# A gated linear-attention layer and its SiLU MLP under a new instruction planner: a modelled transfer queue and PE clock, idle matmuls in thin stretches, four load ranks, four units fed to the MLP one by one

## The chip, the cores and the metric

The kernel runs on one core of one Trainium2 chip. The metric is device time in microseconds (us) of one launch, as the median of several runs. The profile is of one further execution of the same program.

## The reference

There are 4 batches, 8 heads, 768 steps and a head width of 48. Everything is float32 outside the kernel.

```python
f = 1.0 / (1.0 + np.exp(-f_logit))
state = np.zeros((B, H, D, D), dtype=np.float32)
for t in range(S):
    state = f[:, :, t, :, None] * state + np.einsum('bhd,bhe->bhde', k[:, :, t], v[:, :, t])
    y[:, :, t] = np.einsum('bhd,bhde->bhe', q[:, :, t], state)
x = np.ascontiguousarray(y.transpose(0, 2, 1, 3)).reshape(B * S, H * D)   # 3072 x 384
h = x @ w_in                                                              # 384 -> 2048
out = (h * (1.0 / (1.0 + np.exp(-h)))) @ w_out                            # 2048 -> 384
```

The recurrence is computed in chunks of 128 steps, with cumulative sums of the log gates instead of a loop over time.

## The kernel before

**Units.** A unit `u` is one chunk of 128 steps of one batch, all 8 heads; there are 6 chunks times 4 batches, so 24 units, and unit `u` needs the state that unit `u-4` left. Two neighbouring units make a pair `P`, so 12 pairs.

**Steps of a unit**, by the names that the planner gives them (the line is that of the instruction in the kernel before):

- `f k q v` (L390): the four loads, issued by SP. `E`, `L` (L397, L399, ScalarE): log gates from `f`, for both units of a pair at once from pair 2 on.
- `cs` (L445, L449, TensorE): cumulative sums. `ia`, `al`, `a` (L452, L456, L454, ScalarE): three exponentials of them.
- `ki` (L458, GpSimd): k times `ia`. `qg` (L462, VectorE): q times `a`. `vb` (L460, GpSimd): v in bf16.
- the transpose of both: for units 0 to 7 `tq` on TensorE (L468) and a copy `qkc` on VectorE (L470), from unit 8 on `qkD`, a transposing transfer issued by SP (L472).
- `sc` (L479): scores, `at` (L483, VectorE): masked, `y` (L488, L492): the output of the unit, `yc` (L496, VectorE): in bf16.
- its transpose into `xT`: `yT` and `xc` (L502, L504) for units 0 to 7, `xD` from unit 8 on (a transposing transfer, SP, L498).
- `d`, `sd`, `su` (L510, L515 or L517, L521): the next state, on TensorE, VectorE, GpSimd.

**Steps of a pair in the MLP.** `mi` (L426) is a first product: 2 of 16 column tiles of `w_in` for 256 rows, 6 matmuls; 8 of them for a pair. `si` (L422, ScalarE) takes the SiLU of each into `hT`. `mo` (L436) is a quarter of the second product of one unit, 4 matmuls with 128 rows; 4 of them for a unit, in order. `oc` (L439, VectorE) copies the result and `so` (L442) stores it, from GpSimd's queue, for the last units from SP's. `wi` and `wo` (L409, L412) are the weight loads, four quarters each, issued from GpSimd's queue.

**What sets the order.** Nothing is left to a scheduler on the chip. `make_tasks` lists the steps with a duration each, their inputs and their buffers; `schedule` plays them through a model of the engines at build time and picks, on each engine, the ready step with the lowest rank (`pace` times the unit plus the rank of the step's kind). `planned` sorts the steps by the start that the model gave, and they are emitted in that order inside `tc.manual_schedule()`. So each engine runs its own list strictly in order, and waits at the head of the list whenever the model was too hopeful. Buffers are assigned by the model too (`SLOTS`): the PSUM class `mlp`, which holds the results of `mi` and `mo` and of the idle matmuls, has 3 buffers; `cs`, `sc`, `tq` and `yd` have one each.

**ScalarE's two tables.** `exp`/`ln` steps and `si` steps need different function tables, so an `ACT_TABLE_LOAD` is emitted wherever the list changes kind. `hold_...` and `keep_...` are the model's rules for when to change.

**Idle matmuls.** `warm` (L414) multiplies a zero tile into an `mlp` buffer. Before, 70 of them have the lowest priority from the start on, so they fill TensorE's first gaps, and the last is planned ahead of unit 0's `yT`.

**Weights.** `w_after=(2, 2, 2, 3, 3, 3, 4, 5)` ties each of the eight weight loads to the `ki` of a unit.

Of the kernel before, what the change touches and what calls it, by code (L numbers as in the profile page):

```python
# [21 lines left out]
NTILES = 16  # L22

CFG = dict(
    turned=8,
    turned_y=8,
    warm=70,
    warm_at=5.0,
    single=0,
    w_after=(2, 2, 2, 3, 3, 3, 4, 5),  # L30
    pace=3.66,
    margin=0.2,
    late_store=18,
    keep_exp=117.43,
    keep_silu=245.53,
    hold_exp=0.58,
    hold_silu=0.64,
    rank=dict(ld=-44.14, E=-215.27, cs=-365.49, ia=97.44, ki=-23.12, vb=175.4, qg=451.56, tq=-142.94, qkc=-77.52, sc=-74.11, at=-79.38, y=-7.63, yc=-223.81, yT=-176.78, xc=-369.47, d=13.22, sd=-254.14, su=26.79, mi=-117.59, si=-4.81, mo=20.95, mstep=0.47, oc=215.45, so=524.34, wi=23.7, wo=55.81),
# [5 lines left out]
ENGINES = ("PE", "ACT", "DVE", "POOL", "SP")  # L44
SEM = {"PE": 0.22, "ACT": 0.06, "DVE": 0.06, "POOL": 0.08, "SP": 0.0}
INTO_PE = 0.09
TABLE = 1.29


class Task:  # L50
    def __init__(self, name, eng, occ, lat, prio, deps=(), acq=(), use=(), mode=None, dma=0.0):
        self.name, self.eng, self.occ, self.lat, self.prio = name, eng, occ, lat, prio
        self.deps, self.acq, self.use, self.mode, self.dma = list(deps), list(acq), list(use), mode, dma
# [6 lines left out]

def make_tasks(cfg):
    T, tasks, pace, R = {}, [], cfg["pace"], cfg["rank"]
    extra = cfg.get("extra", {})

    def add(name, eng, occ, lat, prio, **kw):
        t = Task(name, eng, occ, lat, prio + extra.get(name, 0.0), **kw)
        T[name] = t
        tasks.append(t)
        return t
# [8 lines left out]
    base = lambda u: pace * u  # L78
    for n in range(cfg["warm"]):
        add(("warm", n), "PE", 0.107, 0.107, 1e6 + n, acq=[inst(("wm", n), "mlp")])  # L80
    for u in range(UNITS):
        P = u // 2
        for n, x in enumerate("fkqv"):
            add((x, u), "SP", 0.45, 0.45, base(u) + R["ld"] + n * 0.1, acq=[inst((x, P), x)], dma=0.875)

    for P in range(PAIRS):
        us_list = [(2 * P,), (2 * P + 1,)] if P < 2 else [(2 * P, 2 * P + 1)]
        for us in us_list:
            occ, lat = (0.43, 0.54) if len(us) == 1 else (0.74, 0.85)
            e = add(("E", us), "ACT", occ, lat, base(us[0]) + R["E"], deps=[T["f", u] for u in us], acq=[inst(("e", us), "e")],  # L90
                    use=[I["f", P]], mode="exp")
            add(("L", us), "ACT", occ, lat, base(us[0]) + R["E"] + 0.1, deps=[e], acq=[inst(("lf", P), "lf")],
                use=[I["e", us]], mode="exp")
    log_of = lambda u: T["L", (u,)] if u < 4 else T["L", (u - u % 2, u - u % 2 + 1)]

    for u in range(UNITS):
        c, b, P, B = u // BATCHES, u % BATCHES, u // 2, base(u)
# [5 lines left out]
        occ = 0.162 + (0 if last else 0.1)  # L103
        cs = add(("cs", u), "PE", occ, occ, B + R["cs"], deps=[log_of(u)], acq=[I["cs", u]], use=[I["lf", P]])
        ia = add(("ia", u), "ACT", 0.387, 0.49, B + R["ia"], deps=[cs], acq=[I["ia", u]], use=[I["cs", u]], mode="exp")
        if not last:
            al = add(("al", u), "ACT", 0.08, 0.173, B + R["ia"] + 0.1, deps=[cs], acq=[I["al", u]], use=[I["cs", u]], mode="exp")
        a = add(("a", u), "ACT", 0.387, 0.486, B + R["ia"] + 0.2, deps=[ia], use=[I["cs", u]], mode="exp")
        ki = add(("ki", u), "POOL", 0.94, 0.994, B + R["ki"], deps=[ia, T["k", u]], acq=[I["qk", u]], use=[I["ia", u], I["k", P]])
        vb = add(("vb", u), "POOL", 0.445, 0.503, B + R["vb"], deps=[T["v", u]], acq=[I["vb", u]], use=[I["v", P]])  # L110
        qg = add(("qg", u), "DVE", 0.47, 0.554, B + R["qg"], deps=[a, T["q", u]], acq=[I["qk", u]], use=[I["cs", u], I["q", P]])
        if u >= cfg["turned"]:
            qkT = add(("qkD", u), "SP", 0.6, 0.6, B + R["tq"], deps=[qg, ki], acq=[I["qkT", u]], use=[I["qk", u]], dma=1.3)
        else:
            tq = add(("tq", u), "PE", 0.444, 0.444, B + R["tq"], deps=[qg, ki], acq=[I["tq", u]], use=[I["qk", u]])
            qkT = add(("qkc", u), "DVE", 0.61, 0.692, B + R["qkc"], deps=[tq], acq=[I["qkT", u]], use=[I["tq", u]])
        sc = add(("sc", u), "PE", 0.425, 0.33, B + R["sc"], deps=[qkT], acq=[I["sc", u]], use=[I["qkT", u]])
        at = add(("at", u), "DVE", 1.2, 1.29, B + R["at"], deps=[sc], acq=[I["atm", u]], use=[I["sc", u]])
        yd = [at, vb] + ([T["su", u - BATCHES]] if c else [])
        y = add(("y", u), "PE", 0.38 if c else 0.21, 0.38 if c else 0.21, B + R["y"], deps=yd, acq=[I["y", u]],  # L120
                use=[I["atm", u], I["vb", u], I["qkT", u]] + ([I["st", u - BATCHES]] if c else []))
        yc = add(("yc", u), "DVE", 0.475, 0.558, B + R["yc"], deps=[y], acq=[I["yb", u]], use=[I["y", u]])
        if u >= cfg["turned_y"]:
            xc = add(("xD", u), "SP", 0.4, 0.4, B + R["yT"], deps=[yc], acq=[I["xT", P]], use=[I["yb", u]], dma=0.6)
        else:
            yT = add(("yT", u), "PE", 0.167, 0.167, B + R["yT"], deps=[yc], acq=[I["yT", u]], use=[I["yb", u]])
            xc = add(("xc", u), "DVE", 0.27, 0.358, B + R["xc"], deps=[yT], acq=[I["xT", P]], use=[I["yT", u]])
        T["x", u] = xc
        if not last:
            d = add(("d", u), "PE", 0.168, 0.168, B + R["d"], deps=[ki, vb, y], acq=[I["d", u]], use=[I["qk", u], I["vb", u]])  # L130
            sdd = [d] + ([T["su", u - BATCHES]] if c else [])
            sd = add(("sd", u), "DVE", 0.464, 0.551, B + R["sd"], deps=sdd, acq=[I["sd", u]],
                     use=[I["d", u]] + ([I["st", u - BATCHES]] if c else []))
            add(("su", u), "POOL", 1.01, 1.07, B + R["su"], deps=[sd, al], acq=[I["st", u]], use=[I["sd", u], I["al", u]])

    for n in range(4):
        add(("wi", n), "POOL", 0.8, 0.8, R["wi"] + n, deps=[T["ki", cfg["w_after"][n]]], dma=2.36)
    for n in range(4):
        add(("wo", n), "POOL", 0.8, 0.8, R["wo"] + n, deps=[T["ki", cfg["w_after"][4 + n]]], dma=2.5)

    for P in range(PAIRS):
        B = base(2 * P + 1)
        single = P < cfg["single"]
        for j in range(NTILES // 2):
            us = [(2 * P + i,) for i in range(2)] if single else [(2 * P, 2 * P + 1)]
            pass
        parts = [(2 * P,), (2 * P + 1,)] if single else [(2 * P, 2 * P + 1)]
        per = 4 if single else 2
        done = {}
        for us in parts:  # L150
            for j in range(NTILES // per):
                h = inst(("h", us, j), "mlp")
                deps = [T["x", u] for u in us] + [T["wi", (j * per) // 4]]
                off = 0.0 if len(us) == 2 else (us[0] - 2 * P - 1) * pace
                mi = add(("mi", us, j), "PE", 0.655, 0.655, B + off + R["mi"] + j * R["mstep"] * per / 2, deps=deps,
                         acq=[h], use=[I["xT", P]])
                done[us, j] = add(("si", us, j), "ACT", 0.476, 0.597, B + off + R["si"] + j * R["mstep"] * per / 2, deps=[mi],
                                  acq=[I["hT", P]], use=[h], mode="silu")
        for i in range(2):
# [3 lines left out]
            for m in range(4):  # L163
                need = [done[us, m]] if single else [done[us, 2 * m], done[us, 2 * m + 1]]
                mo = add(("mo", u, m), "PE", 0.648, 0.648, B + R["mo"] + (4 * i + m) * R["mstep"],
                         deps=need + [T["wo", m]] + ([T["mo", u, m - 1]] if m else []), acq=[o], use=[I["hT", P]])
            oc = add(("oc", u), "DVE", 0.468, 0.552, B + R["oc"] + 4 * i, deps=[mo], acq=[inst(("ob", u), "o")], use=[o])
            late = u >= cfg["late_store"]
            add(("so", u), "SP" if late else "POOL", 0.35 if late else 0.58, 0.5, B + R["so"] + 4 * i, deps=[oc], use=[I["ob", u]],
                dma=0.6)  # L170
# [3 lines left out]
def schedule(tasks, slots, cfg, fixed=None):  # L174

    margin = cfg["margin"]
    for i, t in enumerate(tasks):
        t.idx, t.start, t.end, t.succ, t.ready, t.left = i, None, None, [], 0.0, len(t.deps)
    for t in tasks:
        for d in t.deps:  # L180
            d.succ.append(t)
        for x in dict.fromkeys([*t.acq, *t.use]):
            x.users, x.slot = 0, None
    for t in tasks:
        for x in dict.fromkeys([*t.acq, *t.use]):
            x.users += 1
    free = {c: [(0.0, s) for s in range(n)] for c, n in slots.items()}
    busy = dict.fromkeys(ENGINES, 0.7)
    busy["PE"], busy["ACT"], busy["POOL"] = 1.3, 2.0, 1.9
    waiting = {e: [t for t in tasks if t.eng == e and not t.deps] for e in ENGINES}  # L190
    at = dict.fromkeys(ENGINES, 0)
    st = dict(mode="exp", last=2.0)
    ring = {"SP": [], "POOL": []}
# [386 lines left out]
```

## Time and profile before

| what | value |
|---|---|
| median of 3 runs | 204.59 us (204.46 to 205.04) |
| the profiled execution | 205.16 us |
| its span, first to last instruction | 203.3 us |
| TensorE busy (matmuls, overlapping ones counted once) | 179.0 us |
| ScalarE, VectorE, GpSimd busy | 121.3, 87.3, 72.5 us |
| mean granted TensorE clock | 0.938 |
| moved by DMA | 32.80 MB, 161 GB/s over the span |
| `ACT_TABLE_LOAD` | 16, 1283 ns each |

How to read it: "busy" counts a matmul from its start to its modelled end, and consecutive matmuls overlap, so 179.0 us is more than TensorE needs for this work at full speed. What a group of matmuls really costs is read from the chain of waits, where 60 `mi` matmuls in a row took 6.55 us and 24 `mo` matmuls 3.90 us: 0.655 us for one `mi` step of 6, 0.65 us for one `mo` step of 4. The profiled execution took 205.16 us, 1.86 us more than its span and 0.57 us more than the median of the runs.

### The profile page before, as it was taken

The page shows a single profiled execution, that of the slowest core. Times are in us where ns is not written, and L with a number is a line of the kernel's source. Part 1 is how long each engine was busy: PE and PEld are TensorE (multiplying, and loading weights), DVE is VectorE, ACT ScalarE, POOL GpSimd, SP SyncE. Part 2 cuts the span into 40 slices and gives each one's busy share as a digit, 9 for nine tenths or more (in the row PEclk, how much of TensorE's full clock was granted, in tenths as well). Part 3 has the DMA queues.
Part 4 walks back from the last instruction along what each step waited for, and adds up shares of the span by engine and source line. Part 5 has one row for each costly group of instructions (what it writes and reads, how often), then busy time and mean ns, then how long its engine had stood idle before and what let it go on. Part 6 is the DMA issues. An engine that isn't in the chain of part 4 may idle for free.

```text
span 203.3 us, 4480 instructions
## 1 busy us (share of the span) xinstructions
PE 179.0 (88%) x1766; PEld 131.1 (64%) x1766; DVE 87.3 (43%) x170; ACT 121.3 (60%) x208; POOL 72.5 (36%) x122
## 2 busy tenths in 40 slices
PE   7985889946999999969998997669979999999992
PEld 5764568734687678648567864438748678867850
DVE  4279261037264753872723064233845561162021
ACT  4646228962278769867739966186759767801700
POOL 2449603152181573383047004491167151000000
PEclk9997579995599999999999999969999999999998
DMA  6999999999999699999897999889899294003012
GB/s 133 204 193 173 191 189 195 204 200 187 204 221 236 120 166 247 197 185 191 175 221 156 161 194 187 188 187 213 160 234 156 80 115 112 0 16 118 25 42 77
DMA packets 129140, 32.80 MB, mean 161 GB/s; under 512 B 123904, under 2 KB 128256, under 8 KB 129120
## 3 DMA queue, kind: packets, MB, share of 16 engines
q1 hardware_dynamic: 124256, 25.83, 70.2%
q0 software_dynamic: 4864, 6.69, 14.8%
q8 instruction: 14, 0.23, 0.5%
q14 instruction: 6, 0.05, 0.1%
HBM read 25.17 MB, written 4.72 MB: 147 GB/s over the span
## 4 chain that ended last, share of the span: by engine, by line
PE 57%; DMA 13%; SPq 6%; ACT 3%; issue 2%; DVE 2%; POOL 0%; DVEq 0%; ACTq 0%
PE mlp L426 26%; PE mlp L436 23%; DMA f<-in_f_logit_dram 5%; SPq L390 5%; DMA xT<-yb 4%; DMA w_out_sb<-in_moe_w_out_dram 3%; PE sc L479 2%; PE yd L488 2%; ACT e L397 1%; PE yd L492 1%; PE cs L445 1%; SPq L498 1%; DVE qk L462 1%; DVE o L439 1%; PE yd L510 1%
## 5 line engine op out<-in xcount | busy, mean ns | idle before, releaser
L422 ACT ACTIVATE hT<-mlp 128x512 bf16<-128x512 f32 x96 | 56.6, 597 | 27.9 <-PE mlp L426 23.9
L436 PE MATMUL mlp<-w_out_sb,hT 128*128 128x384 bf16 x384 | 71.6, 333 | 1.8 <-DMA w_out_sb<-in_moe_w_out_dram 1.8
L426 PE MATMUL mlp<-xT,w_in_sb 128*128 128x256 bf16 x576 | 69.9, 280 | 2.7 <-DMA xT<-yb 1.3
L426 PEld LDWEIGHTS <-w_in_sb 128*128 128x128 bf16 x576 | 56.6, 100 | 12.6 <-DMA xT<-yb 2.0
L483 DVE TENSOR_TENSOR atm<-sc,triu 128x512 bf16<-128x512 f32 x48 | 30.9, 685 | 45.0 <-PE sc L479 44.8
L436 PEld LDWEIGHTS <-hT 128*128 128x128 bf16 x384 | 35.4, 99 | 22.8 <-issue 3.3
L458 POOL TENSOR_TENSOR qk<-k,ia 128x384 bf16<-128x384 f32 x24 | 23.9, 997 | 29.8 <-ACT al L456 22.2
L452 ACT ACTIVATE ia<-cs 128x384 f32<-128x384 f32 x24 | 11.7, 489 | 26.4 <-PE cs L449 20.5
L460 POOL CAST vb<-v 128x384 bf16<-128x384 f32 x24 | 12.0, 503 | 42.4 <-DMA v<-in_v_dram 29.5
L521 POOL TENSOR_TENSOR st<-sd,al 48x192 bf16<-48x192 f32 x40 | 20.1, 502 | 18.5 <-DVE sd L515 9.6
L462 DVE TENSOR_TENSOR qk<-q,cs 128x384 bf16<-128x384 f32 x24 | 13.2, 550 | 24.3 <-ACT cs L454 23.5
L439 DVE COPY o<-mlp 128x384 f32<-128x384 f32 x24 | 13.2, 554 | 18.6 <-PE mlp L436 18.5
L549 ACT ACT_TABLE_LOAD x15 | 19.2, 1283 | 0.3
L397 ACT ACTIVATE e<-f 128x768 f32<-128x768 f32 (+1 forms) x14 | 10.5, 750 | 14.6 <-DMA f<-in_f_logit_dram 14.6
L445 PE MATMUL cs<-lf,triu 128*128 128x384 bf16 x24 | 8.1, 339 | 9.9 <-DVE qk L462 6.6
L496 DVE CAST yb<-yd 128x384 bf16<-128x384 f32 x24 | 13.3, 552 | 6.7 <-PE yd L492 5.1
L449 PEld LDWEIGHTS <-lf 128*128 128x128 bf16 x80 | 5.0, 98 | 12.3 <-issue 10.7
L442 POOL DMA_DIRECT2D out_dram<-o x18 | 10.4, 580 | 5.3 <-DVE o L439 4.1
L454 ACT ACTIVATE cs<-cs 128x384 f32<-128x384 f32 x24 | 11.4, 477 | 0.6
L515 DVE TENSOR_TENSOR sd<-yd,st 128x384 f32<-128x384 f32 x16 | 8.8, 552 | 6.9 <-issue 2.9
L479 PE MATMUL sc<-qkT 48*128 48x128 bf16 x192 | 10.4, 233 | 1.1 <-DVE qkT L470 1.0
L414 PE MATMUL mlp<-idle 128*128 128x256 bf16 x70 | 10.1, 299 | 1.1 <-DVE idle L533 1.1
(35 smaller groups left out, 112.3 us busy)
## 6 DMA issues: line engine op xcount, KB each, us to landing
f<-in_f_logit_dram SPq DMA_DIRECT2D x24, 192.0 KB, 3.9
k<-in_k_dram SPq DMA_DIRECT2D x24, 192.0 KB, 4.1
q<-in_q_dram SPq DMA_DIRECT2D x24, 192.0 KB, 4.0
v<-in_v_dram SPq DMA_DIRECT2D x24, 192.0 KB, 4.0
out_dram<-o POOLq DMA_DIRECT2D x18, 192.0 KB, 3.7
w_in_sb<-in_moe_w_in_dram POOLq DMA_DIRECT2D x4, 384.0 KB, 9.1
w_out_sb<-in_moe_w_out_dram POOLq DMA_DIRECT2D x4, 384.0 KB, 9.5
out_dram<-o SPq DMA_DIRECT2D x6, 192.0 KB, 2.0
```

The source lines that it names most:

```text
L397: nc.scalar.activation(e, at("f", u // 2)[:, i:i + n], AF.Exp, scale=-1.0)
L422: return nc.scalar.activation(at("hT", P)[:, per * j:per * (j + 1), lo:hi], h, AF.Silu)
L426: nc.tensor.matmul(h[:, i, :], w_in_sb[:, kk, n * 128:(n + 1) * 128], at("xT", P)[:, kk, lo:hi], start=(kk == 0), stop=(kk == KT - 1))
L436: nc.tensor.matmul(o, at("hT", P)[:, n, i * C:(i + 1) * C], w_out_sb[:, n, :], start=(n == 0), stop=(n == NT - 1))
L439: nc.vector.tensor_copy(at("ob", u), at("o", u)[:, 0:d_model])
L458: nc.gpsimd.tensor_mul(at("qk", u)[:, 1, :, 0:D], at("k", P)[:, i], at("ia", u))
L462: nc.vector.tensor_mul(at("qk", u)[:, 0, :, 0:D], at("q", P)[:, i], at("cs", u)[:, 0:HD].rearrange("p (h d) -> p h d", d=D))
L479: nc.tensor.matmul(a_ps[:, r, p, :], qkT[lo:lo + D, 1, p, :], qkT[lo:lo + D, 0, p, :], start=True, stop=True)
L483: nc.vector.tensor_mul(at("atm", u)[:, r], at("sc", u)[:, r], triu[:, None, :].to_broadcast([C, NP, C]))
L496: nc.vector.tensor_copy(at("yb", u), at("y", u))
L521: nc.gpsimd.tensor_mul(at("st", u)[lo:lo + D, :, r * D:(r + 1) * D], at("sd", u)[lo:lo + D, :, r * D:(r + 1) * D], at("al", u)[lo:lo + D, ...
L549: nc.scalar.preload_act_table_set(tables[turn[id(t)]])
```

## The change

The arithmetic, the tiles, the buffers and the bytes moved are the same. The planner is replaced, and with it the order of every engine's list. Its core:

```diff
 CFG = dict(
-    turned=8,
-    turned_y=8,
-    warm=70,
-    warm_at=5.0,
-    single=0,
-    w_after=(2, 2, 2, 3, 3, 3, 4, 5),
-    pace=3.66,
-    margin=0.2,
+    single_logs=2,
+    single=2,
     late_store=18,
...
+    turned=range(8, 24),
+    turned_y=range(8, 24),
+    rank=dict(ldf=-50.7, ldk=16.34, ldq=10.3, ldv=40.31, E=114.29, cs=24.58, ia=-464.65, ki=-1093.0, vb=499.5, qg=-627.06,
...
+    rel={"wi_0": 23.29, "wi_1": 19.57, "wi_2": 16.93, "wi_3": 17.83, "wo_0": 14.71, "wo_1": 26.85, "wo_2": 38.7, "wo_3":
+         41.24},
+    pace=31.54,
...
+LOAD = dict(ring=0, svc=0.95, elig=1.2, land=0.75)
+QKD = dict(ring=0, svc=1.25, elig=1.25, land=1.1)
...
-            add((x, u), "SP", 0.45, 0.45, base(u) + R["ld"] + n * 0.1, acq=[inst((x, P), x)], dma=0.875)
+            add((x, u), "SP", 0.62, 0.62, "ld" + x, u, off=n * 0.1, acq=[inst((x, u // 2), x)], dma=LOAD)
...
-        if u >= cfg["turned"]:
-            qkT = add(("qkD", u), "SP", 0.6, 0.6, B + R["tq"], deps=[qg, ki], acq=[I["qkT", u]], use=[I["qk", u]], dma=1.3)
+        if u in cfg["turned"]:
+            qkT = add(("qkD", u), "SP", 1.25, 1.25, "qkD", u, deps=[qg, ki], acq=[I["qkT", u]], use=[I["qk", u]], dma=QKD)
...
-        add(("wi", n), "POOL", 0.8, 0.8, R["wi"] + n, deps=[T["ki", cfg["w_after"][n]]], dma=2.36)
+        add(("wi", n), "POOL", 0.8, 0.8, "wi", off=n, dma=W_IN)
...
+    def wants_warm():
+        if WARM_FROM <= now < WARM_ALL:
+            return True
+        past = now - win
+        return now < WARM_TO and clock > 0.6 and past > 0.8 and load_of(win, now) < WARM_SHARE * past
...
+        while win + WINDOW <= now + 1e-9:
+            share = load_of(win, win + WINDOW) / WINDOW
+            clock = 1.0 if share >= UP else 0.5 if share <= DOWN else clock
+            win += WINDOW
```

The constants are the planner's own; they act on the chip only through the order they lead to. That order, read from the two built programs:

- **SP.** Before, the loads go unit by unit as `f k q v`. After, they go by four ranks: `f:0 f:1 q:0 f:2 k:0 v:0 q:1 f:3 k:1 v:1 q:2 f:4 k:2 v:2 q:3 f:5 k:3 v:3 q:4 f:6 k:4 v:4 ...`, so `f` runs two units ahead of `k` and `v`, and `q` one. Before, the last load `v:23` is issued ahead of `xD:17`; after, in a steady pattern such as `f:17 k:15 v:15 q:16 f:18 xD:13 k:16 v:16 qkD:15 q:17 xD:14 qkD:16`, and the last load `v:23` stands behind `qkD:22` and `xD:20`.
- **GpSimd.** Weight loads before: `... vb:2 wi:0 wi:1 wi:2 ki:3 su:0 wi:3 wo:0 su:1 wo:1 vb:3 su:2 su:3 vb:4 vb:5 ki:4 wo:2 ki:5 vb:6 wo:3`. After: `... ki:1 vb:1 wo:0 ki:2 vb:2 su:0 wi:2 wi:3 su:1 wi:1 ki:3 su:2 wi:0 wo:1 vb:3 su:3 ki:4 vb:4 wo:2 ki:5 wo:3`.
- **ScalarE.** `E L ia al a` of unit 4 now come ahead of the first table load. There are 19 table loads between the kinds instead of 15: from pair 4+5 to pair 18+19 ScalarE changes to the exponentials and back around the 8 `si` steps of every pair, where before pairs 10+11 and 12+13 shared one stretch, and so did the last three pairs (after, the last two do).
- **TensorE.** 77 idle matmuls instead of 70, the last of them ahead of unit 3's `tq`. Units 0 to 3 pass the first product one by one (`single=2`): 4 steps each of 12 matmuls with 128 rows, in the order in which the quarters of `w_in` are asked for. From pair 8+9 on the list repeats, as here: `cs:17 y:15 sc:16 mo:12,0 d:12 mo:12,1 mo:12,2 mo:12,3 mo:13,0 mo:13,1 cs:18 y:16 mi:14+15,0 mi:14+15,1 d:13 mo:13,2 mo:13,3 mi:14+15,2 mi:14+15,3 mi:14+15,4 sc:17 mi:14+15,5 mi:14+15,6 mi:14+15,7 cs:19 y:17 ...`.

## Prediction before the run

> **What bounds the kernel now.** I first read the page's 40 slices, one digit for each 5.08 us.
>
> ```profile
> PE   7985889946999999969998997669979999999992
> ...
> PEclk9997579995599999999999999969999999999998
> DMA  6999999999999699999897999889899294003012
> ```
>
> TensorE looks busy nearly everywhere, DMA until slice 31. But the clock falls to half around 18 to 28 us and 46 to 56 us, and DMA's busy share is no proof of saturation: the page's GB/s row moves between 120 and 247 in those slices. So I asked how much of TensorE's time is work at full rate. The chain of waits gives prices where matmuls follow each other without a gap, and the places where they do not:
>
> ```profile
> 31.14 6.55 PE mlp L426 x60
> 37.69 3.90 PE mlp L436 x24
> ...
> 43.43 6.76 DMA w_out_sb<-in_moe_w_out_dram
> ...
> 86.11 5.03 DMA xT<-yb
> ...
> 101.08 3.18 DMA xT<-yb
> ...
> 128.53 3.48 DMA f<-in_f_logit_dram
> ```
>
> A `mi` step of 6 costs 0.655 us and a `mo` step of 4 costs 0.65; other rows of the chain give `cs` 0.24, `sc` 0.33, `y` 0.37 to 0.48 (I take 0.40), `d` 0.17 to 0.28 (0.2), `tq` 0.45, `yT` 0.17. A pair from unit 8 on is 8 x 0.655 + 8 x 0.65 + 2 x 1.17 = 12.8 us of TensorE. Between the first `mi` of pair 4+5 (58.21 us) and that of pair 22+23 (186.34 us) lie 72 `mi` and 72 `mo` steps (47.2 + 46.8) and the small steps of 18 units (20.8): 114.8 us of work in 128.1 us, so 13.3 us lost, in the DMA waits above and in waits for a late `f`. The three waits in the chain from 86 us on are of one sort: SP's list is in order, and what is needed next stands behind something that is waiting, or behind loads that nobody needs yet. Ahead of 58 us the view by windows (columns: length, PE busy, clock, DMA share, GB/s) shows the other loss:
>
> ```profile
> 42.00:46.00 4.00, 1.59 (x23) 0.85 1.01 195
> 46.00:50.00 4.00, 2.31 (x28) 0.50 1.22 190
> 50.00:54.00 4.00, 3.76 (x24) 0.50 1.27 215
> ...
> 152.00:186.30 34.30, 34.30 (x341) 1.00 0.48 89
> ```
>
> From 37.7 to 58.2 us TensorE does 11.7 us of work (12 `mo`, four `cs`, two each of `tq`, `sc`, `y`, `yT`, one `d`): it runs out of work at 41.6, waits for the third quarter of `w_out`, then works at a clock of 0.50. From 152 us on it is full at clock 1.00 while DMA has half its load or less: a backlog that the first 150 us left. The kernel is bound by TensorE, starved of inputs for its first three quarters.
>
> **The change, part by part.** I sum against the profiled execution, 205.16 us: 203.30 of span and 1.86 around it, 0.57 above the median.
>
> *Weights and start.* The first `mi` runs at 22.05 now, on a quarter of `w_in` issued at 15.21 (6.8 us to landing, the shortest of its four). In the new list `wi:2`, the first one needed, stands behind `vb:2` and `su:0`. `v:2` is the 14th load instead of the 12th, and `wo:0` (twice a load's bytes) goes ahead of it: four load times of 0.90 us (the 11 load issues from 34.95 to 44.88 us) after `vb:2`'s 14.76, then `su:0` for 1.1: issue near 19.5, landing 26.3 to 28.6 us. So the first products start 4 to 6 us later. They then have 16 steps, 10.5 us: end 37 to 40 us, against 37.69; I take 39. In that gap only 77 instead of 70 idle matmuls, 0.107 us each at full rate, keep the clock; I count no gain.
>
> *Single first products.* 12 matmuls of 128 rows take the place of 6 of 256. No row shows them; the nearest is `tq`, 8 transposes with a new weight tile each in 0.45 us, so 0.67 us a step, +0.2 us over 16 steps. The upper bound is one weight load each, not overlapped (99 ns): 1.19 us a step, +8.5 us. A gain is excluded, since the same columns stream. I take the `tq` row, which has the same shape; and part of it would hide behind the arrival of `w_in`.
> The Trainium skill speaks against this edit: "TensorE: Matmul & The Clock Gate", section "Back-to-back issue gap", gives about 81 ns for 128-column matmuls in a stream of load and matmul. By it the 16 steps would cost 16 x (12 x 0.081 - 0.655) = 5 us more instead of 0.2, an estimate. The trace's 56 ns a transpose is below that, so I stay with the row.
>
> *The third and fourth quarter of `w_out`.* Now issued at 43.43 and 46.12, behind `ki:4` and `ki:5`, which wait for the table change and `cs:4`. In the new list ScalarE does unit 4's exponentials ahead of the SiLUs, so `ki:4`, `vb:4` wait only for their loads. `v:4` is the 22nd load; the 20th and 24th landed by 35.9 and 39.5 us (the two `vb` rows that waited for them) behind the same number of weight quarters, six. So `wo:2` goes out near 38.2, `wo:3` after `k:5` near 42.2; landing 45.0 and 49.0 by the 6.8 us row. TensorE has 6.7 us of work from 39 on (6 `mo`, two each of `tq`, `cs`, `sc`, one each of `y`, `d`, `yT`); at 45.7 the third quarter is there, three `mo`, a `y` and a `cs` take it to 48.3, the fourth comes at 49.0, and after three `mo` and a `yT` pair 4+5 can begin at 51.1. If the thin stretch halves the clock again, as the window rows show, add 2 to 3 us. I take 52.7 against 58.21: a gain of 5.5, bounds 0 and 7.
>
> *The steady list.* Each pair now has its turn of exponentials and its turn of SiLUs. ScalarE's bill for a pair: 8 SiLUs of 0.60, two units of 0.49 + 0.17 + 0.48, `E` and `L` of 0.84, two table loads of 1.28: 11.3 us, under TensorE's 12.8. The four added table loads cost 5.1 us of ScalarE, hidden behind the `mo` steps of the pair before. If that cover goes, a pair costs up to 1.3 us more. What a table change costs beyond the load:
>
> ```profile
> 116.44 1.91 ACT L422 ACTIVATE hT<-mlp 128x512 bf16<-128x512 f32 x3
> 118.37 1.28 ACT L549 ACT_TABLE_LOAD   x1
> 119.66 0.84 ACT L397 ACTIVATE e<-f 128x768 f32<-128x768 f32 x1
> ```
>
> The next activation starts 0.01 us after the load, so 1.3 us in all.
> The Trainium skill ("ScalarE: Activation LUTs", "What ACT_TABLE_LOAD costs") puts a switch at about 2.66 us with a drain. By that, as an estimate, ScalarE would need 14.1 us for a pair and the sum below would rise by 9 x (14.1 - 13.4) = 6 us. The rows above show no drain.
>
> The new wait: `cs` of the even unit stands on TensorE behind six `mo` steps and needs the `L` of the same turn; behind it are queued that pair's `y` and `mi`, and ScalarE's SiLUs wait for these. The rows "cs waits for lf" hold 3.4 us in 6 cases, 0.57 each; one a pair for 9 pairs is 5.1 us. Where the old losses go: `f` is issued two units earlier than its `k` and `v`, so the waits for `f` should end; `xD` and `qkD` have fewer unneeded loads ahead. What is late next is `xD`: issued after `yc`, median 3.4 us to landing (2.3 to 5.0), and in the list some 4 us of other TensorE work lie between.
>
> SP's own bill for a pair is bounded: 8 loads of 0.6 and four transposing issues of 1.3 make 10.0 us of pure issue; with loads at the 0.90 us that the transfers took and two stores at the same price it is 14.2. I take 12.4, the loads at 0.90 and stores hidden, since only the first is paced by a ring that was full.
>
> *Sum.* 52.7; work of the stretch 114.8, and two `mo` steps of unit 21 that now lie ahead, 1.3; waits 5.1: pair 22+23 begins at 173.9 (now 186.34). Then 8 `mi` and 10 `mo`, 11.7: 185.6. From the last matmul to the end 3.9, as now: span 189.5, plus 1.86: 191.4, and 190.8 for the median.
>
> **The rivals.** *Slower: SP's list becomes the bound.* Loads are now nearly just in time, and a transposing transfer that waits at the head of SP's list holds back `k` and `v` of the next units. In the view of waits for SP's queue it waited 16.1 us ahead of the 16 `qkD` and 15.1 us ahead of the 16 `xD`, one wait of 12.7 us near the end left out: 1.0 us each. Now the loads issued ahead cover that. Four such waits on top of 10.0 us are 14.0 us a pair, on top of 12.4 they are 16.4; at the middle, 15.2, 9 x (15.2 - 13.4) = 16 us more than my sum: 207. It decides from 14.9 us a pair. For it speaks that the last load goes out at 147.56 us now with `xD:17` still behind it, and that reserve is given up; against it, that the GB/s row reaches 247 while its mean up to 157 us is near 190, so there is capacity to catch up.
>
> *The start gains nothing* (clock at half, `w_out` no earlier): 5.5 us more, 196.3. *DMA paces each pair at 14.2 us*: 9 x 0.8 to 1.0, about 199. *Both, so no change worth the name*: the steady loss stays 13.3 and the start stays, 204.5.
>
> **How the numbers follow.** My forecast 0.53; late start 0.14; DMA pace 0.11; no change 0.03; SP bound 0.19. Faster by over 0.3% (about what a measurement of this kernel can tell from none): 0.53 + 0.14 + 0.11 = 0.78; the same 0.03; slower 0.19. The low end is the start at 51.1 and no `cs` waits, 190.8 - 1.6 - 5.1 = 184; the high end takes in the no-change case and the milder half of the SP case, a pair up to 15.1 us: 206.
>
> **What would show it.** Right: first `mi` later than 22 us, pair 4+5 at 51 to 54 us, the slices around 50 us without a second half-clock dip, `mi` of pair 22+23 near 174 us, table loads each followed at once. Wrong: waits of `mi` for `xT` or of `vb` and `ki` for loads in every pair, pairs over 14.9 us apart, or a clock of 0.5 behind 56 us.

## The result and the profile after

The kernel went from 204.81 us (median of 4 runs beside it, 204.46 to 205.94) to 195.46 us (195.17 to 198.47): a ratio of 0.953, 95% interval 0.948 to 0.958, a gain of 9.3 us by the medians. I had said 190.8, in a range of 184 to 206, and faster with a chance of 0.78.

Runs more than 1.5% above the fastest of the same kernel are left out of every ratio and of the means in the table below; the profiled executions of the changed kernel (198.47 us) and of `e2_half_loads` are such runs. So I read the first profile (196.7 us of span) together with a second and a third one of the same kernel, from `e1_again` (192.0 us of span) and `e9_again` (193.2), and call a cost settled only where they agree. First the page's 40 slices of the first profile, one digit for each 4.92 us:

```profile
PE   7785669999999999959999979988999899999991
...
PEclk9999699999999999978999999999999999999998
DMA  6999999799999797998989798999999795422001
```

The first dip of the clock is still there, in slice 5: the clock is granted at half from 21.3 to 24.8 us. The second one, from 45 to 55 us, is gone. What is new is a fall to 7 in slice 18, behind a wait of 2.0 us for `qkT`; in the other two profiles the longest such wait is 1.0 us, and there is no such fall. The view by windows (length, TensorE busy, clock, DMA share, GB/s) answers the rows that I had shown of before:

```profile
42.00:46.00 4.00, 4.00 (x44) 1.00 1.18 177
46.00:50.00 4.00, 3.52 (x49) 1.00 1.28 222
50.00:54.00 4.00, 4.00 (x47) 1.00 0.99 190
152.00:180.00 28.00, 27.05 (x265) 1.00 0.57 125
```

TensorE was busy for 1.59 and 2.31 us of the first two of these windows before, and at half clock from 46 us on. Now it is busy for 4.00 and 3.52 us, at the full clock. GpSimd's timeline (start, us, step, and in brackets the idle time ahead of it) shows why: the last two quarters of `w_out` go out at 40.08 and 44.04 us instead of 43.43 and 46.12. `ki:4`, ahead of the first of them, now waits for its load `k` and no longer for ScalarE; `ki:5`, ahead of the second, still waits 2.20 us for ScalarE.

```profile
38.70 1.00 POOL L496 TENSOR_TENSOR qk<-k,ia 128x384 bf16<-128x384 f32 x1 [1.03 <-DMA k<-in_k_dram]
...
40.08 0.80 POOL L450 DMA_DIRECT2D w_out_sb<-in_moe_w_out_dram  x1
43.09 0.99 POOL L496 TENSOR_TENSOR qk<-k,ia 128x384 bf16<-128x384 f32 x1 [2.20 <-ACT al L494]
44.04 0.80 POOL L450 DMA_DIRECT2D w_out_sb<-in_moe_w_out_dram  x1
```

What the prediction missed is in the steady stretch. The chain of waits of the second profile (start, us, what; transposing transfers only):

```profile
76.65 6.15 DMA qkT<-qk
...
91.85 3.80 DMA xT<-yb
...
105.60 4.55 DMA xT<-yb
...
123.36 5.23 DMA qkT<-qk
...
134.51 2.77 DMA xT<-yb
...
151.30 5.71 DMA qkT<-qk
```

Six transposing transfers lie on the path here, and no late `f`. In the other two profiles it is five and four of them, beside late loads: a `v`, a `k` and an `f` (4.14 us) in the first, a `v` and a `k` in the third. And TensorE's waits between 52 and 181 us, second profile (total, times, longest):

```profile
PE sc L517 <- DMA qkT<-qk: 2.7, 5, 1.0
PE mlp L464 <- DMA xT<-yb: 2.4, 3, 1.3
```

No `cs` waits for `L` here, the wait that I had priced at 5.1 us; nor does one in the other two profiles. The first profile has 3.4 and 3.4 us in the first two rows, and one `qkD` of 7.22 us at 78.31, behind which the clock is granted at half from 86.2 to 89.6 us. In the kernel before, the same view over the stretch has no wait for `qkT` and for `xT` only this:

```profile
PE mlp L426 <- DMA xT<-yb: 1.3, 2, 1.0
```

So these waits have grown with the change. Its largest waits there were others, 4.8 us of `cs` for VectorE and 2.0 us of `cs` for a late `L`; of these the second profile has none in the stretch.

All runs in one table. The second column is a mean. "Start" is the first `mi` of pair 4+5, "stretch" the time from there to the first `mi` of pair 22+23, "last" the end of the last matmul, in us of the profile. The sets differ by up to 2% (the kernel before took 201.0, 204.8 and 203.7 us in the three), so totals of different sets are compared by the ratio to before, and kernels of one set by their means. A ratio is not exactly the quotient of the means: for e1, e2 and e3 that quotient is 0.961, 0.930 and 1.050, for the others it lies within 0.002 of the ratio.

| kernel | mean us | ratio, 95% | start | stretch | last |
|---|---|---|---|---|---|
| before | 205.01 | 1 | 58.2 | 128.0 | 199.4 |
| after | 195.36 | 0.953 (0.948, 0.958) | 52.6 | 128.2 | 192.7 |
| e1_again | 193.09 | 0.954 (0.947, 0.962) | 51.3 | 124.7 | 187.9 |
| e2_half_loads | 186.86 | 0.925 (0.916, 0.933) | 53.9 | 118.3 | 184.1 |
| e3_loads_ahead | 211.12 | 1.045 (1.033, 1.056) | 49.9 | 144.6 | 206.4 |
| e4_unit4_late | 202.47 | 1.007 (1.003, 1.012) | 61.1 | 122.6 | 195.7 |
| e5_transfers_first | 201.10 | 0.981 (0.970, 0.991) | 53.7 | 130.4 | 196.0 |
| e6_pairs_first | 197.36 | 0.964 (0.955, 0.972) | 56.3 | 124.9 | 193.1 |
| e7_no_idle | 193.16 | 0.943 (0.934, 0.952) | 53.4 | 123.2 | 188.5 |
| e8_before_early4 | 208.04 | 1.016 (1.007, 1.024) | 62.7 | 127.5 | 203.4 |
| e9_again | 194.50 | 0.955 (0.948, 0.963) | 51.9 | 125.4 | 189.2 |
| e10_no_idle_again | 193.10 | 0.948 (0.940, 0.956) | 53.1 | 123.2 | 188.2 |
| e11_v_on_gpsimd | 197.08 | 0.969 (0.963, 0.975) | 52.9 | 127.2 | 192.0 |
| e12_before_f_ahead_early4 | 204.61 | 1.005 (1.000, 1.009) | 58.0 | 128.2 | 199.4 |

e1 to e4, e5 to e8 and e9 to e12 each ran on one chip, side by side. How far a single start can be trusted shows in the column: after, e1, e2, e3, e5, e9 and e11 have the same lists up to there, and pair 4+5 begins anywhere from 49.9 to 53.9 us.

Beside the 58.2 and 128.0 us of before, the three profiles of the changed kernel gain 5.6 to 6.9 us at the start, 0 to 3.3 us in the stretch and 1.3 us behind it, where two `mo` fewer are left (the upper ends are those of `e1_again`, on the faster chip).

### The profile page after: what moved, and what is told of

Same layout as the page of the kernel before. It is cut to its first block, busy times and chain, and to the rows that moved or that the text cites. A ratio compares the mean times of both kernels' runs of the same rounds, so it can differ in the third digit from the quotient of the medians.

```text
span 196.7 us, 4677 instructions
## 1 busy us (share of the span) xinstructions
PE 175.4 (89%) x1869; PEld 131.1 (67%) x1869; DVE 89.1 (45%) x170; ACT 125.7 (64%) x212; POOL 72.6 (37%) x122
## 4 chain that ended last, share of the span: by engine, by line
PE 49%; DMA 26%; SPq 8%; ACT 6%; POOL 4%; issue 3%; DVE 2%; POOLq 0%; DVEq 0%
PE mlp L464 25%; PE mlp L474 17%; DMA qkT<-qk 9%; SPq L428 6%; DMA v<-in_v_dram 6%; DMA w_in_sb<-in_moe_w_in_dram 5%; DMA xT<-yb 3%; ACT L587 3%; PE sc L517 2%; DMA f<-in_f_logit_dram 2%; DMA k<-in_k_dram 2%; POOL st L559 2%; ACT e L435 1%; DVE o L477 1%; SPq L536 1%
## 5 line engine op out<-in xcount | busy, mean ns | idle before, releaser
L464 PE MATMUL mlp<-xT,w_in_sb 128*128 128x256 bf16 (+1 forms) x672 | 70.5, 261 | 5.4 <-DMA xT<-yb 3.4
L474 PE MATMUL mlp<-w_out_sb,hT 128*128 128x384 bf16 x384 | 69.0, 326 | 0.0
L464 PEld LDWEIGHTS <-w_in_sb 128*128 128x128 bf16 x672 | 57.3, 99 | 14.4 <-issue 4.3
L534 DVE CAST yb<-yd 128x384 bf16<-128x384 f32 x24 | 13.4, 557 | 25.4 <-PE yd L530 25.4
L490 ACT ACTIVATE ia<-cs 128x384 f32<-128x384 f32 x24 | 11.8, 490 | 16.1 <-PE cs L487 13.1
L500 DVE TENSOR_TENSOR qk<-q,cs 128x384 bf16<-128x384 f32 x24 | 13.2, 552 | 16.8 <-ACT cs L492 11.9
L498 POOL CAST vb<-v 128x384 bf16<-128x384 f32 x24 | 12.1, 503 | 21.4 <-DMA v<-in_v_dram 21.0
L517 PE MATMUL sc<-qkT 48*128 48x128 bf16 x192 | 9.7, 222 | 4.4 <-DMA qkT<-qk 3.4
L452 PE MATMUL mlp<-idle 128*128 128x256 bf16 x77 | 12.7, 313 | 1.1 <-DVE idle L571 1.1
L517 PEld LDWEIGHTS <-qkT 48*128 48x128 bf16 x192 | 5.5, 95 | 8.9 <-DMA qkT<-qk 4.2
L437 ACT ACTIVATE lf<-e 128x768 bf16<-128x768 f32 (+1 forms) x14 | 10.4, 745 | 0.2
## 6 DMA issues: line engine op xcount, KB each, us to landing
f<-in_f_logit_dram SPq DMA_DIRECT2D x24, 192.0 KB, 4.0
q<-in_q_dram SPq DMA_DIRECT2D x24, 192.0 KB, 4.0
k<-in_k_dram SPq DMA_DIRECT2D x24, 192.0 KB, 3.9
v<-in_v_dram SPq DMA_DIRECT2D x24, 192.0 KB, 4.1
out_dram<-o POOLq DMA_DIRECT2D x18, 192.0 KB, 3.7
out_dram<-o SPq DMA_DIRECT2D x6, 192.0 KB, 1.9
```

The source lines that it names most:

```text
L452: return nc.tensor.matmul(at("warm", rest[0])[:, 0:256], idle[:, 0:128], idle, start=True, stop=True)
L464: nc.tensor.matmul(h[:, i, :], w_in_sb[:, kk, n * 128:(n + 1) * 128], at("xT", P)[:, kk, lo:hi], start=(kk == 0), stop=(kk == KT - 1))
L474: nc.tensor.matmul(o, at("hT", P)[:, n, i * C:(i + 1) * C], w_out_sb[:, n, :], start=(n == 0), stop=(n == NT - 1))
L500: nc.vector.tensor_mul(at("qk", u)[:, 0, :, 0:D], at("q", P)[:, i], at("cs", u)[:, 0:HD].rearrange("p (h d) -> p h d", d=D))
L517: nc.tensor.matmul(a_ps[:, r, p, :], qkT[lo:lo + D, 1, p, :], qkT[lo:lo + D, 0, p, :], start=True, stop=True)
L534: nc.vector.tensor_copy(at("yb", u), at("y", u))
```

## The experiments

In e1 and e9 the changed kernel runs as it is; in e2 the size of the loads is edited (it leaves out half of the input of units 12 to 23, so it is no kernel to use), in all others the lists of the built program. What is not named stays as planned.

**What is left in the stretch: the transposing transfers and the loads.** First the kernel itself again, for the spread between executions.

> The changed kernel as it is, for a second profile. In its first profile (198.47 us, 3.0 us above the median of the other three runs) the stretch from the first mi of pair 4+5 to that of pair 22+23 took 128.2 us (52.77 to 180.95), as long as before (128.1), where my sum had 121.2. Theory A (the stretch lost the 7 us to waits for transfers that differ from run to run): about 195.3 us, the stretch 124 to 126 us, the first 52.8 us the same within 0.3. Rival (the first 52.8 us differ): the stretch stays at 128 and the start moves by 3.

Measured: the stretch took 124.7 us here and 125.4 in `e9_again`, against 128.2 in the first profile. The waits for transposing transfers are 5.1, 5.4 (whole span) and 6.8 us, so they do differ from run to run, but they are there every time. The start was 0.7 to 1.3 us earlier as well, more than the 0.3 that I had allowed.

Then with half the bytes:

```diff
-        nc.sync.dma_start(out=at(x, u // 2)[:, u % 2], in_=SRC[x]...[b, c * C:(c + 1) * C])
+        n = H if u < 12 else H // 2
+        nc.sync.dma_start(out=at(x, u // 2)[:, u % 2, 0:n], in_=SRC[x]...[b, c * C:(c + 1) * C, 0:n])
```

> Every load of units 12 to 23 moves only heads 0 to 3 (half of the bytes and packets; the other heads keep what the buffer had from twelve units before); all lists and all issues stay. Theory B, the DMA engines are simply full: about half of the 48 late loads' time is given back, the waits of sc for qkT and of mi for xT behind pair 10+11 go, and the time falls by 5 to 8 us, to 187 to 190. Theory A2, the order in SP's list (a transfer that waits at its head holds what is behind it): the waits at the head stay, only landings get a little earlier, 1 to 2 us off: 193.5 to 194.5.

Measured: 186.9 us, 6.2 less than `e1_again` beside it, and a stretch of 118.3 us, 2.2 above the 116.1 us of matmul work that I had counted (114.8 and the two moved `mo`). From pair 12+13 to pair 20+21 the pairs follow each other every 12.9 us (109.6 to 161.3 us, four pairs), my 12.8 of TensorE alone. TensorE's waits of that stretch, 52 to 181 us:

```profile
PE mlp L475 <- DMA w_out_sb<-in_moe_w_out_dram: 0.7, 1, 0.7
...
PE mlp L465 <- DMA xT<-yb: 0.2, 1, 0.2
```

The order of SP's list is the same, and so is the number of transfers in it; only the loads are smaller, half of the bytes in half of the packets. Beside `e1_again` the DMA share fell from 0.95 to 0.82 (84 to 116 us) and from 0.98 to 0.70 (116 to 148), the landing of `qkD` from a median of 4.2 to 3.2 us, of `xD` only from 2.8 to 2.7. So the loss that the stretch still has goes with the size of the loads. By what way is not separated: behind 84 us a load also held SP for 0.59 us on average instead of 0.83, so SP's list moved faster as well, and no run here makes the issues shorter without making the transfers smaller.

Could another order of the list help? Two runs moved the balance, one each way:

```diff
- SP, after:  k:14 v:14 qkD:13 q:15 xD:12 qkD:14 f:17 k:15 v:15 q:16 f:18 xD:13
+ SP, e3:     k:14 v:14 xD:10 q:15 xD:11 qkD:13 f:17 k:15 v:15 q:16 f:18 xD:12
- SP, after:  q:14 f:16 xD:11 k:14 v:14 qkD:13 q:15 xD:12 qkD:14 f:17
+ SP, e5:     q:14 xD:11 f:16 k:14 qkD:13 v:14 xD:12 qkD:14 q:15 f:17
```

> In SP's list every load moves ahead of up to two transposing transfers; the order among the loads and among the transfers stays, and so do all other lists. Theory A2 (order): k and v of the next units land earlier, GpSimd's waits for k and v shrink, qkD goes out earlier: 2 to 4 us faster than the changed kernel, 191 to 193.5. Theory B (DMA full): each transposing transfer now has more loads ahead of it, sc and mi wait longer: 0 to 3 us slower, 195 to 198.

> In SP's list every transposing transfer up to the last f moves ahead of the one load in front of it; all else stays. Theory D (what a pair loses over its 12.8 us of TensorE work is the time that qkD and xD stand behind loads in the ring; putting loads ahead of them cost 21 us): each is issued about one load, 0.9 us, earlier, the waits of sc for qkT and of mi for xT shrink, 1 to 3 us faster than the changed kernel. Rival (the order in SP's list is balanced: the load that is passed now waits behind a transfer that waits for its data): k and v come later, ki and qkD with them, 0 to 3 us slower.

Measured for loads ahead: 211.1 us, 18.0 more than `e1_again` and far above the 0 to 3 us of theory B. The stretch takes 144.6 us, and it is one wait that does it (the same view, whole span):

```profile
PE sc L569 <- DMA qkT<-qk: 14.6, 5, 5.1
```

Each such wait empties TensorE, and the mean granted clock is 0.90 to 0.95 in the windows 50 to 84, 84 to 116, 116 to 148 and 148 to 194 us, against 1.00 in `e1_again` up to the last matmuls. For transfers first: 201.1 us, and 0.981 against about 0.954 is some 5.5 us slower than the changed kernel. Here the waits for transfers stay small (1.8 and 1.8 us), and others take their place (first two rows). The chain of waits leads them back to late loads: an `f` ahead of the 1.3 us of `cs`, a `v` ahead of the 2.1 us of `y` (last two rows).

```profile
PE yd L568 <- POOL st L601: 2.6, 2, 2.1
PE cs L525 <- DVE qk L542: 2.4, 3, 1.3
...
74.80 3.39 DMA f<-in_f_logit_dram
...
95.96 4.36 DMA v<-in_v_dram
```

So one list has both kinds of lateness to share out, and the planned order lies between. Of the two orders tried, one in each direction, both are worse.

The last one takes loads out of SP's list instead:

```diff
- SP:      ... k:12 qkD:11 v:12 q:13 ... k:13 v:13 q:14 ...
+ SP:      ... k:12 qkD:11 q:13 ... k:13 q:14 ...
- GpSimd:  ... vb:6 ki:7 vb:7 vb:8 so:3 ...
+ GpSimd:  ... vb:6 v:12 ki:7 vb:7 v:13 vb:8 v:14 so:3 ...
```

> The v loads of units 12 to 23 go out from GpSimd's list, six units ahead of their vb, so SP's list keeps three loads and two transposing transfers per unit. Theory (the stretch loses its 4 to 8 us because transposing transfers stand behind loads in one list and one ring): the waits sc for qkT and mi for xT shrink from some 5 us in all to under 1.5 us, and the kernel is 2 to 5 us faster than the changed one (190 to 193 where that takes 195). Rival (any load that moves beside a transposing transfer slows it, whoever issues it; or twelve more descriptor-building issues hold up ki and vb on GpSimd): the same within 1 us, or slower by up to 5 us with new waits for GpSimd's steps.

Measured: 197.1 against 194.5 us beside it, 2.6 slower, with intervals that just meet. The two halves of the stretch went opposite ways. Behind 118 us, where only two of the twelve moved loads are left, no wait of TensorE remains and the way from pair 12+13 to pair 22+23 takes 62.8 us instead of 65.9. Ahead of it `sc` waits 5.8 us for `qkD` (once 3.4) instead of 1.3, and pair 8+9 starts 4.2 us later than in `e9_again`, 1.0 of it there from the start. I had put the moved loads six units ahead, so ten of the twelve go out before 118 us; the median landing of `xD` over the whole run rose from 3.2 to 4.3 us. So taking them out of SP's list did not help where they moved earlier. That it is the moving beside a transposing transfer that counts, whoever issues the load, fits this and e2, but was not shown by itself. A later issue of the same loads was not tried.

**Where the 5.6 to 6.9 us at the start come from.** Undo one part: unit 4's exponentials behind the first SiLUs again.

```diff
- ACT:  ... a:3 E:4+5 L:4+5 ia:4 al:4 a:4 si:0,2 ... si:3,3 ia:5 ...
+ ACT:  ... a:3 si:0,2 ... si:3,3 E:4+5 L:4+5 ia:4 al:4 a:4 ia:5 ...
- PE:   ... sc:2 warm warm cs:4 warm ... mi:3,3 cs:5 mo:0,0 ...
+ PE:   ... sc:2 warm warm warm ... mi:3,3 cs:4 cs:5 mo:0,0 ...
```

> Undoes one part of the start: on ScalarE E, L of pair 4+5 and ia, al, a of unit 4 go behind the first 16 SiLUs again (as in the kernel before), with cs:4 on TensorE ahead of cs:5. Theory C (the start's gain of 5.4 us comes from ki:4 no longer waiting for the table change, which lets the third and fourth quarter of w_out out earlier): ki:4 comes some 6 us later, wo:2 near 46 instead of 40.1, pair 4+5 begins 4 to 6 us later, 199 to 201 in all. Rival (it comes from the weights' and loads' new order alone): at most 1 us slower, below 196.5.

Measured: 202.5 us, 9.4 more than `e1_again`, and the start is 9.8 later, where I had expected 4 to 6. From its timeline:

```profile
44.12 0.32 PE L527 MATMUL cs<-lf,triu 128*128 128x384 bf16 x1 [3.71 <-ACT lf L481]
45.24 0.99 POOL L540 TENSOR_TENSOR qk<-k,ia 128x384 bf16<-128x384 f32 x1 [7.60 <-ACT al L538]
...
46.63 0.80 POOL L494 DMA_DIRECT2D w_out_sb<-in_moe_w_out_dram  x1
46.75 2.72 PE L518 MATMUL mlp<-w_out_sb,hT 128*128 128x384 bf16 x8
```

`ki:4` waits 7.60 us for ScalarE, the third quarter of `w_out` goes out 6.5 us later than in the first profile, and TensorE, idle for 3.71 us at `cs:4`, then does 8 matmuls in 2.72 us that take 1.46 at the full rate: the second dip is back. The undo costs more than the gain. A likely reason, which was not tested, is that I put `cs:4` ahead of six `mo` that could have run; in the kernel before they run first. So the run shows that the gain hangs on the early turn, and not how much of the 9.8 us does.

Then the other way: that part alone, put into the kernel before, and once more with `f` two units ahead of `k q v`.

```diff
- ACT:     ... a:3 si:0+1,0 ... si:2+3,7 E:4+5 L:4+5 ia:4 al:4 a:4 ia:5 ...
+ ACT:     ... a:3 E:4 L:4 ia:4 al:4 a:4 si:0+1,0 ... si:2+3,7 E:5 L:5 ia:5 ...
- GpSimd:  ... vb:4 vb:5 ki:4 wo:2 ki:5 vb:6 wo:3 ...
+ GpSimd:  ... vb:4 ki:4 wo:2 vb:5 ki:5 wo:3 vb:6 ...
- PE:      ... mi:0+1,1 sc:3 y:2 mi:0+1,2 ... mo:2,1 cs:4 cs:5 ...
+ PE:      ... mi:0+1,1 sc:3 y:2 cs:4 mi:0+1,2 ... mo:2,1 cs:5 ...
```

and in e12 alone, up to unit 11:

```diff
- SP:      f:0 k:0 q:0 v:0 f:1 k:1 q:1 v:1 f:2 k:2 ...
+ SP:      f:0 f:1 f:2 k:0 q:0 v:0 f:3 k:1 q:1 v:1 f:4 k:2 ...
```

> The kernel before with one part of the change: on ScalarE E, L, ia, al, a of unit 4 (alone, 384 columns) go ahead of the first SiLUs, cs:4 on TensorE ahead of the third mi, and on GpSimd ki:4 and wo:2 ahead of vb:5, wo:3 ahead of vb:6; pair 4+5's E and L become two each. Theory C (the start's gain is this): wo:2 goes out at 36 to 38 us instead of 43.4, pair 4+5 begins 3 to 5 us earlier than in the kernel before, and the total falls by 2 to 5. Rival (the start's gain needs the loads' new ranks and the weights' order too): pair 4+5 within 1 us of before, total within 1 us.

> The kernel before with three things of the change together: unit 4's exponentials ahead of the first SiLUs, ki:4 and wo:2 ahead of vb:5 and wo:3 ahead of vb:6, and (new against the run that was slower) f issued two units ahead of k, q, v up to unit 11. Theory (the move on ScalarE pays only once f:4 is there in time): the wait of E:4 for f, 10.7 us without this, falls under 2 us, wo:2 goes out before 41 us, pair 4+5 begins at 52 to 56 us instead of 58 to 62, and the kernel is 2 to 6 us faster than the one before (199 to 203). Rival (the start is lost to something else, or what is gained is given back at pair 10+11, where the old list shares one stretch of tables): pair 4+5 at 58 or later, or the total within 1 us of the kernel before.

Measured for the part alone: 208.0 us, 1.6% slower than before. From its timeline:

```profile
29.50 0.52 ACT L462 ACTIVATE e<-f 128x384 f32<-128x384 f32 x1 [10.69 <-DMA f<-in_f_logit_dram]
30.63 0.48 PE L510 MATMUL cs<-lf,triu 128*128 128x384 bf16 x1 [3.55 <-ACT lf L464]
32.37 1.28 ACT L614 ACT_TABLE_LOAD   x1
```

In the unit by unit order `f:4` is the 17th load; ScalarE stands 10.69 us for it with all first SiLUs queued behind. The first products end at 47.2 us instead of 37.5.

With `f` ahead: 204.6 us, no gain, and pair 4+5 at 58.0. Of my theory the wait for `f:4` held and the sum did not. ScalarE's longest wait for an `f` is 3.1 us, `wo:2` goes out at 40.35, and from the end of the first products to pair 4+5 it takes 14.9 us (43.08 to 58.00) instead of 20.7 (37.53 to 58.21): 5.8 us gained there. But the first products end 5.5 us later. Of this 1.6 us is there at the first `mi` (23.61 instead of 22.05 us), whose quarter of `w_in` goes out 1.8 us later, behind `vb:2`, whose load is now the 14th instead of the 12th. Most of the rest hangs on `cs:4`: its input `L:4` is ready at 19.7 us, but in TensorE's list I had put it behind two `mi`, `sc:3` and `y:2`, and ScalarE waits for it with all first SiLUs queued behind, so that the first of them runs at 29.70 us instead of 23.54:

```profile
27.33 0.49 ACT L520 ACTIVATE ia<-cs 128x384 f32<-128x384 f32 x1 [7.61 <-PE cs L517]
...
30.35 1.44 PE L494 MATMUL mlp<-xT,w_in_sb 128*128 128x256 bf16 x6 [2.44 <-ACT hT L490]
```

TensorE then waits for a SiLU and runs six matmuls in 1.44 us, 0.82 at the full rate; the clock is granted at half from 29.7 to 36.5 us. In the changed kernel the first products end at 40.4 and 38.8 us (first profile, `e9_again`), 2.9 and 1.3 later than before, and 12.2 and 13.1 us after that pair 4+5 begins. There `cs:4` stands ahead of all first products. So the gain at the start needs the early exponentials (undone, they cost all of it), and in the old lists they gave nothing in the two forms that I tried; the old lists with `cs:4` ahead of all first products were not tried.

**First products one by one, and the idle matmuls.**

```diff
- PE:  mi:0,2 mi:1,2 sc:3 mi:2,2 mi:0,3 mi:1,3 mi:2,3 y:3 mi:0,1 ... mi:3,2 mi:3,3 cs:5
+ PE:  mi:0+1,4 mi:0+1,5 sc:3 mi:0+1,6 mi:0+1,7 mi:0+1,2 mi:0+1,3 y:3 mi:0+1,0 mi:0+1,1 yT:3 d:3 mi:2+3,0 ... mi:2+3,7 cs:5
```

> The first products of pairs 0+1 and 2+3 in steps of 6 matmuls with 256 rows again, in the places of the 16 single steps; pair 2+3 therefore wholly after pair 0+1, with unit 3's yT and d ahead of it; all other lists stay. If the single steps fill the waits for the quarters of w_in, TensorE waits for w_in instead, has 10 steps instead of 7 left when the last quarter lands, and pair 4+5 begins 1.5 to 2.5 us later. The steps themselves get 0.3 to 0.6 us cheaper in all. Rival (the start is bound by ki:4 and the last quarters of w_out anyway): within 0.5 us of the changed kernel.

Measured: ratio 0.964 against 0.953 to 0.955, about 2 us slower, the intervals overlapping. Pair 4+5 begins at 56.3 us, behind the 49.9 to 53.9 of the unchanged start. TensorE's waits (whole span):

```profile
PE mlp L524 <- DMA w_in_sb<-in_moe_w_in_dram: 3.7, 3, 1.9
```

Three units one by one give TensorE 2.1 us of work for each quarter of `w_in` that arrives, a pair only 1.3 us, so in pairs TensorE waits at each of the next three quarters. The gain of the single steps fits that, but in the total it is at the edge of what the runs can tell.

The idle matmuls left out, in two sets:

```diff
- PE:  warm warm ... cs:0 warm ... (77 of them)
+ PE:  cs:0 cs:1 tq:0 ...
```

> All 77 idle matmuls left out, all else stays. Theory E (they keep the granted clock up until the first products): the clock falls to half before 28 us, the first steps of mi run at half for up to 3.4 us, 1 to 3 us slower. Rival (the first 28 us are bound by loads and by w_in, not by TensorE): the first mi at the same time and the total within 0.7 us.

> The 77 idle matmuls left out, beside the changed kernel this time. Theory (idle matmuls keep TensorE's rate up for the first products): the first products end later, pair 4+5 at 53.4 as in the earlier run without them, and the kernel is 1 to 2 us slower than the changed one. Rival (the start is bound by the loads and the quarters of w_in, so the rate before 31 us is worth nothing): within 0.7 us of it; a gain of over 1 us would mean that they cost something, and the place would have to be found.

Measured: ratios 0.943 and 0.948, against 0.954 and 0.955 for the kernel with them; beside it on one chip 193.1 against 194.5 us, with overlapping intervals. In the total they give nothing that can be measured, and taking them out may gain 1 us; a better version than the changed kernel is not shown. The matmuls that they were to speed up are slower without them: the first 24 single products take 1.51 us in the first profile (first row) and 2.74 in `e7_no_idle`.

```profile
28.30 1.51 PE L464 MATMUL mlp<-xT,w_in_sb 128*128 128x128 bf16 x24 [1.54 <-DMA w_in_sb<-in_moe_w_in_dram]
...
27.30 2.74 PE L501 MATMUL mlp<-xT,w_in_sb 128*128 128x128 bf16 x24 [0.42 <-DMA w_in_sb<-in_moe_w_in_dram]
```

The start moves by 1.2 us beside `e9_again` (53.1 against 51.9), within the spread of starts above, and the stretch then is 2.2 us shorter; why was not looked into.

## Why the prediction was right, and where its sum was off

**The start** held, step by step. The first `mi` came at 28.3 us (first profile), 27.0 and 26.1 (foretold 26.3 to 28.6), the first products ended at 40.4 and 38.8 (39), pair 4+5 began at 52.6, 51.3 and 51.9 (52.7). `wo:2` and `wo:3` went out at 40.08 and 44.04 us in the first profile, 1.9 and 1.8 later than I said, and at 37.92 and 42.42 in `e9_again`. The second dip at half clock went. What I named as the cause, ScalarE's early turn, is necessary (e4) and, in the two forms tried in the old lists, not sufficient (e8, e12). I had priced the load order as a cost of the first products alone, while it also feeds the early turn: with `f` behind, ScalarE stood 10.69 us for it (e8), with `f` ahead at most 3.1 (e12).

**Single first products** cost 0.69 us a step where 84 matmuls follow each other, foretold 0.67:

```profile
35.75 4.82 PE mlp L464 x84
```

That is 57 ns a matmul. The Trainium skill's 81 ns ("TensorE: Matmul & The Clock Gate", "Back-to-back issue gap") is not seen here, and with it the 5 us that an estimate from it had put on this edit. "A gain is excluded" was written of the step alone; that single steps fill the waits for the quarters of `w_in`, to which e6 points, was not in the sum.

**Table loads** follow at once, and are followed at once:

```profile
71.79 1.91 ACT L460 ACTIVATE hT<-mlp 128x512 bf16<-128x512 f32 x3 [0.49 <-PE mlp L464]
73.72 1.28 ACT L587 ACT_TABLE_LOAD   x1
75.01 0.49 ACT L490 ACTIVATE ia<-cs 128x384 f32<-128x384 f32 x1
```

The 19 loads never made ScalarE the bound: with the loads' bytes halved, pairs came at TensorE's own 12.9 us with all table loads in place (e2). The drain in the skill's 2.66 us ("ScalarE: Activation LUTs", "What ACT_TABLE_LOAD costs") does not show: 0.02 us lie ahead of the load above and 0.01 behind it.

**The stretch** is the term that failed. I foretold 121.2 us: 116.1 of work and 5.1 of waits. It took 128.2, 124.7 and 125.4: 8.6 to 12.1 us above the work. The wait that I put in, `cs` for the `L` of its own turn, did not come: in the three profiles the `L` of a pair ended ahead of its `cs`, for the first three pairs by only 0.05 to 0.26 us, later by 0.4 to 2.2. What I had taken for cured came instead: I wrote that `xD` and `qkD` have fewer unneeded loads ahead, counted the stalls for them as gone, and named `xD` only as what is late next, at no price. They cost 5.1 to 6.8 us of waits in the three profiles. That this is near the 5.1 us in my sum is luck, for I had put those down for another wait. The row for it stood in my own text: DMA full up to slice 31 and bytes unchanged, so a transposing transfer that is issued just in time can land among loads. The rest of the excess, 3.5 to 5.3 us, is not put to named waits. With the loads' bytes halved the total excess is 2.2 us, so most of it goes with them too.

**The tail** held: 11.9 us from the `mi` of pair 22+23 to the last matmul (foretold 11.7), 4.0 from there to the end (3.9), 1.8 around the span.

**The rivals.** SP's list as the bound, 207 us: not in the changed order. Its mechanism, a transfer at the head of the list that holds back loads, is nearer to what e5 shows, at some 5.5 us; in e3, at 211.1 us, it is the transfers that are late. Either way the order has little slack. DMA as the pace, 14.2 us a pair: in `e1_again` pairs 8+9 to 20+21 came every 13.65 us (83.2 to 165.1, six pairs), in the first profile every 14.0, between my 13.4 and that rival's 14.2. e2 speaks for its reason, the amount of data, and the measured 195.46 lies a little nearer to its 199 than to my 190.8. "The start gains nothing" fell. Of the signs that I had named against myself one came once, a clock at half behind 56 us (86.2 to 89.6 us in the first profile); the kernel before has one too, from 133.5 to 136.9 us, and the other two profiles have none up to the last matmuls.

Of the 4.7 us between 190.8 and 195.46, the stretch alone, 3.5 to 7.0 us over, accounts for it.

## What to carry to other kernels

When a change makes transfers just in time while the bytes stay the same and the DMA engines are near full, price the wait behind every transfer on the path, not only its place in the list. A step that opens the way for others (here unit 4's exponentials) pays only with the loads that feed it and with a fitting place in every list that it passes through, so test it undone in the new kernel as well as alone in the old one. Two edits in opposite directions from a planned order show quickly whether it has slack.

## What the runs showed of the hardware

- Without idle matmuls the page's clock row reads 9 in all slices and the mean granted clock is 1.000 (e7), yet the first products run at about half the rate (24 matmuls in 2.74 instead of 1.51 us, the next 48 in 3.65 instead of 2.89), up to about 32 us. The trace's first record of the clock stands at 32.2 us there (30.5 in e10, 4.3 in the first profile of the changed kernel). Ahead of the first record the row reads full and says nothing; the duration of a matmul does.
- A transposing transfer needed a median of 4.2 us (`qkD`) in `e1_again`, beside loads of 192 KB, and 3.2 in e2, where half of the loads were half as large, though its own bytes were the same. The longest in the three profiles of the changed kernel took 7.22 us.
- Loads issued from GpSimd's list cost it 0.93 us each and landed in 4.9 us (median), no sooner than the 3.8 to 4.3 us of SP's loads in the changed kernel beside it.
